# Linear attention into two FFN layers: each head of a pair computes in its own half of the array's columns, the state is kept as diagonal blocks, and the attention's output is cast straight into the FFN's operand

## The chip, the cores and the metric

One core of a Trainium2 chip runs the whole program. The metric is the time on the device in microseconds (us), the median of three runs. The engines are named as the profile names them: PE (TensorE, matmuls; PEld is its loading of weights), DVE (VectorE), ACT (ScalarE), POOL (GpSimd) and SP (SyncE, which here only issues DMAs).

## The reference

Four sequences of 768 steps, 8 heads of 48 features each, pass through an attention with a decaying state; the rows (3072 x 384) then pass through two FFN layers of width 2048.

```python
for t in range(S):
    state = alpha[:, :, t, :, None] * state + np.einsum('bhd,bhe->bhde', k[:, :, t], v[:, :, t])
    y[:, :, t] = np.einsum('bhd,bhde->bhe', q[:, :, t], state)
...
h = x @ w_in;  g = np.maximum(0.01 * h, h);                          x = g @ w_out      # layer 1
h = x @ w_in;  g = np.where(h > 0, h, np.exp(np.minimum(h, 0)) - 1); out = g @ w_out    # layer 2
```

## The kernel before

**Attention.** Time is cut in chunks of 128 steps: 24 units (4 sequences of 6 chunks; `c` is the chunk in its sequence). The 8 heads are 4 pairs (`NP`); the features of a pair's first head lie on partitions 0 to 47, those of the second on 64 to 111 (`PR` = 112). A unit runs through `attn_prep` (products of the decays by two scans on DVE, which scale k and q), `attn_S` (`sc`: scores of each head, on rows 0 to 47 or 64 to 111 of the array; `pk`: k transposed), `attn_S_post` (`A`: masked scores, DVE; `kn`: k copied, ACT; `T`: the old state times the unit's decay), `attn_V` (`po`: output; `pu`: the state's gain) and `attn_V_post`. The state `S` and `T` are [112, 4, 96]: both heads' value columns for every row, of which only the two 48 x 48 blocks on the diagonal are wanted; `mhead`, a column of ones and zeros for each head, clears the others. `vals` holds each pair's values as 48 columns of head 0, 48 zeros and 48 columns of head 1, so that a window of 96 columns that starts at 0 or at 48 places a head's output on rows 0 to 47 or 48 to 95 of `po`.

**Into the FFN.** The FFN wants 384 features as three chunks of 128 partitions (`KD` = 3). Four pairs of 96 features are three chunks of 96 plus a fourth pair, which is cut in three pieces of 32. `attn_V_post` copies `po` into `x32` in that layout with four ACT copies, casts it to `xh` (float32r, ACT), and subtracts to get the rest `xl` (POOL for units 0 to 7, `EARLY_X`, later DVE; `T` likewise with `EARLY_T`).

**FFN.** Every product of layer 1 and 2 is three float32r matmuls (high x high, low x high, high x low). A block is 4 units (512 rows); blocks 0 to 5 of layer 1 run 16 steps each of `ffn1_h` (9 matmuls), `ffn1_g` (ACT, DVE, ACT, DVE) and `ffn1_y` (9 matmuls). While block j runs, the units of block j + 1 run between its steps. `x` tiles have two buffers. The weights come as raw float64 words: `stage1` loads one 128-column step of layer 1 into a slot of `x2t` (four slots), and `convert_p`, `convert_a` and `convert_b` make the high and low parts on ACT and DVE; those of layer 1 run before and during block 0, those of layer 2 during block 5, with rotating pairs of temporaries (`conv_args`: x2t[4] and x2t[5] for layer 1, four pairs of attention tiles for layer 2).

**What sets the order.** Tile's scheduler orders each engine's instructions and places the waits; each engine and each DMA queue then works in its order. PSUM for attention is three banks (`ps_a`), shared by `sc`, `pk`, `po` and `pu`. All loads and stores but one are issued from SP.

## Time and profile before

| | |
|---|---|
| median of 3 runs | 965.43 us (964.12 to 968.95) |
| the profiled execution | 966.94 us, span 965.2 us, granted clock 0.992 |
| PE busy | 931.7 us, 97% of the span |
| DVE, ACT, POOL busy | 57%, 50%, 3% |
| moved by DMA | 54.42 MB, mean 56 GB/s |

The profile is of one execution. PE's busy time counts matmuls in flight, so a busy PE may still run below its best pace; the pace is read from the starts of its rows.

### The profile page before, as it was taken

Reading aid. Unit: us, or ns where it says so; the run is one execution under the profiler, and the core shown is the slowest. Engines: PE = TensorE matmul, PEld = TensorE weight load, DVE = VectorE, ACT = ScalarE, POOL = GpSimd, SP = SyncE. Lnnn points to the kernel's source line nnn. Section 1 sums busy time; section 2 is a strip of 40 time slices with the busy share of each in tenths; the row PEclk is TensorE's granted clock in tenths of the full one; section 3 lists DMA queues with packets and bytes.
Section 4 is the critical chain, followed back from the end, with each engine's and each line's share of the span. In section 5 each row is a group of like instructions: output and inputs, shape, how many; then the busy total and the mean of one; then the engine's idle time right before and its main releaser. Section 6 shows DMA issues by size and latency. Waiting matters only on the chain.

```text
span 965.2 us, 12697 instructions
## 1 busy us (share of the span) xinstructions
PE 931.7 (97%) x4914; PEld 807.6 (84%) x4914; DVE 549.0 (57%) x974; ACT 483.6 (50%) x927; POOL 24.1 (3%) x46
## 2 busy tenths in 40 slices
PE   4889999999999999999999999999999999999997
PEld 3778777888888888888888889989999999999996
DVE  7999999635555557554499973433433433333332
ACT  4566765434334344443488764544544544444442
POOL 0220200000000000000000000000000000000000
PEclk9889999999999999999999999999999999999999
DMA  9445462001112021111144300000000000000001
GB/s 283 124 150 168 130 201 76 1 0 42 42 42 66 18 82 43 42 42 33 55 142 131 115 17 1 6 29 0 33 1 1 34 1 1 33 1 1 34 1 36
DMA packets 17220, 54.42 MB, mean 56 GB/s; under 512 B 1952, under 2 KB 5024, under 8 KB 17152
## 3 DMA queue, kind: packets, MB, share of 16 engines
q1 hardware_dynamic: 17024, 53.31, 17.9%
q8 instruction: 40, 0.66, 0.3%
q14 instruction: 28, 0.23, 0.1%
q10 hardware_dynamic: 128, 0.23, 0.1%
HBM read 48.81 MB, written 4.72 MB: 55 GB/s over the span
## 4 chain that ended last, share of the span: by engine, by line
PE 85%; DVE 10%; DMA 2%; ACT 1%; issue 1%; POOL 0%; SPq 0%; DVEq 0%; ACTq 0%; POOLq 0%
PE hp L312 21%; PE y L283 18%; PE hp L258 18%; PE oa L343 10%; PE o L343 10%; PE po L185 3%; PE sc L155 2%; DMA x2t<-in_w_dram 1%; PE po L188 1%; PE pu L194 1%; DVE x2t L237 1%; DVE E L136 1%; DVE F L140 1%; DVE A L167 1%; DMA pack<-in_seqs_dram 1%
## 5 line engine op out<-in xcount | busy, mean ns | idle before, releaser
L81 DVE TENSOR_TENSOR gl<-t,gh 128x512 fp32r<-128x512 f32 x192 | 132.2, 689 | 109.0 <-ACT gh L78 108.1
L78 ACT CAST gh<-t 128x512 fp32r<-128x512 f32 x192 | 119.1, 621 | 137.6 <-PE oa L343 44.8
L283 PE MATMUL y<-gh,wo 128*128 128x512 f32 x576 | 178.5, 397 | 0.5 <-ACT wo L240 0.5
L321 DVE SCALAR_TENSOR_TENSOR t<-t,hp 128x512 f32<-128x512 f32 x96 | 66.0, 688 | 164.3 <-ACT t L320 164.3
L258 PE MATMUL hp<-xh,wi 128*128 128x512 f32 x576 | 151.2, 395 | 1.2 <-DVE t L267 1.2
L312 PE MATMUL hp<-xh,wi 128*128 128x512 f32 x576 | 149.2, 394 | 0.0
L258 PEld LDWEIGHTS hp<-xh,wi 128*128 128x128 f32 x576 | 107.2, 189 | 24.2 <-ACT wi L240 1.6
L283 PEld LDWEIGHTS y<-gh,wo 128*128 128x128 f32 x576 | 105.7, 188 | 21.9 <-ACT wo L240 1.2
L319 ACT ACTIVATE t<-hp 128x512 f32<-128x512 f32 x96 | 57.3, 597 | 129.1 <-PE hp L312 129.1
L312 PEld LDWEIGHTS hp<-xh,wi 128*128 128x128 f32 x576 | 106.7, 188 | 16.8
L283 PE MATMUL y<-gl,wo 128*128 128x512 f32 x288 | 107.4, 392 | 0.0
L343 PE MATMUL oa<-wo,gh 128*128 128x384 f32 x384 | 98.1, 337 | 0.0
L267 DVE TENSOR_TENSOR t<-t,hp 128x512 f32<-128x512 f32 x96 | 65.3, 680 | 57.3 <-ACT t L266 57.2
L343 PE MATMUL o<-wo,gh 128*128 128x384 f32 x384 | 97.3, 336 | 0.0
L266 ACT ACTIVATE t<-hp 128x512 f32<-128x512 f32 x96 | 57.0, 595 | 78.1 <-PE hp L258 77.6
L312 PE MATMUL hp<-xl,wi 128*128 128x512 f32 x288 | 81.9, 392 | 0.0
L258 PE MATMUL hp<-xl,wi 128*128 128x512 f32 x288 | 81.4, 390 | 0.0
L185 PE MATMUL po<-A,vt 128*96 128x128 f32 x384 | 64.4, 292 | 11.7 <-DVE A L167 11.7
L343 PEld LDWEIGHTS o<-wo,gh 128*128 128x128 f32 x384 | 70.8, 188 | 5.3
L343 PEld LDWEIGHTS oa<-wo,gh 128*128 128x128 f32 x384 | 70.3, 188 | 2.9
L185 PEld LDWEIGHTS po<-A,vt 128*96 128x96 f32 x384 | 52.9, 176 | 16.7 <-DVE A L167 14.0
L312 PEld LDWEIGHTS hp<-xl,wi 128*128 128x128 f32 x288 | 54.1, 188 | 12.5
(106 smaller groups left out, 1124.0 us busy)
## 6 DMA issues: line engine op xcount, KB each, us to landing
pack<-in_seqs_dram SPq DMA_DIRECT2D x23, 674.2 KB, 5.1
x2t<-in_w_dram SPq DMA_DIRECT2D x16, 768.0 KB, 4.9
stg<-in_w_dram SPq DMA_DIRECT2D x28, 384.0 KB, 3.1
vt<-in_vals_dram SPq DMA_DIRECT2D x24, 288.0 KB, 4.5
out_dram<-osb SPq DMA_DIRECT2D x24, 192.0 KB, 1.9
x2t<-in_w_dram SPq DMA_DIRECT2D x4, 384.0 KB, 3.7
pack<-in_seqs_dram SPq DMA_DIRECT2D x1, 226.2 KB, 3.8
pack<-in_seqs_dram ACTq DMA_DIRECT2D x1, 224.0 KB, 4.0
```

Source lines behind the costliest of these rows:

```text
L78: nc.scalar.copy(dst, src)
L81: (lo_engine or nc.vector).tensor_sub(lo, src, dst.bitcast(F32))
L155: nc.tensor.matmul(sc[j][:, p], lhsT=kS[r, p, :], rhs=qh[r, p, :], start=True, stop=True)
L185: nc.tensor.matmul(po[:, p], lhsT=vt[:, p, j * D:j * D + PD], rhs=A[:, j, p], start=(j == 0), stop=(j == 1 and c == 0))
L258: nc.tensor.matmul(hp, lhsT=a[:, kk, :], rhs=x[:, kk, :n], start=(i == 0), stop=(i == 3 * KD - 1))
L266: nc.scalar.activation(t, hp, ACTF.Copy, scale=0.01)
L267: nc.vector.tensor_max(t, t, hp)
L283: nc.tensor.matmul(ytiles[j][c], lhsT=a[:, c * 128:(c + 1) * 128], rhs=x, start=(m == 0 and i == 0), stop=(m == KF - 1 and i == 2),)
L312: nc.tensor.matmul(hp, lhsT=a[:, kk, :], rhs=x[:, kk, :], start=(i == 0), stop=(i == 3 * KD - 1))
L319: nc.scalar.activation(t, hp, ACTF.Relu, scale=-1.0)
L321: nc.vector.scalar_tensor_tensor(out=t, in0=t, scalar=-1.0, in1=hp, op0=ALU.add, op1=ALU.max)
L343: nc.tensor.matmul(otiles[j][i], lhsT=a[:, i * 128:(i + 1) * 128], rhs=x, start=(m == 0 and n == 0), stop=(m == KF - 1 and n == 2),)
```

## The change

Every matmul of `attn_V` is done for each head by itself, with its output on partitions 0 to 47 (or 63) for head 0 and 64 to 111 for head 1, that is in the left or the right 64 columns of the array. `po` is therefore laid out as the heads are, [112, 4, 128]; the matmuls on `T` and for `pu` become 8 for 4. `T` is one constant tile whose blocks off the diagonal are cleared once; only the 48 x 48 blocks are multiplied, and `S` holds those alone ([112, 4, 48]). `mhead` and `x32` are gone. ACT casts `po` into `xh`, DVE subtracts into `xl`; both for every unit, so POOL keeps only a small clearing per unit. The FFN's operand gets a fourth chunk: pairs 0 to 2 lie in chunks 0 to 2 with 16 free partitions behind each head, pair 3 lies in chunk 3, and after the last unit of a block `gather` moves its 96 rows, 16 at a time, into the free partitions: six DMAs for `xh`, six for `xl`. `stage1` brings the rows of w_in into the same order with four DMAs, and w_out with a fifth. Layer 2's conversions have three sets of temporaries for four.

```diff
         if c > 0:
-            T = at_p.tile([PR, NP, PD], F32, tag="T", name="T")
-            (nc.gpsimd if u < EARLY_T else nc.vector).tensor_mul(T, st["S"], d["pe"].to_broadcast([PR, NP, PD]))
-            d["T"] = T
+            for j in range(2):
+                r = slice(64 * j, 64 * j + D)
+                nc.vector.tensor_mul(
+                    T[r, :, j * D:(j + 1) * D], st["S"][r], d["pe"][r].to_broadcast([D, NP, D]))
...
-        po = ps_a.tile([PD, NP, C], F32, tag="at", name="po")
+        po = ps_a.tile([PR, NP, C], F32, tag="at", name="po")
         for p in range(NP):
             for j in range(2):
-                nc.tensor.matmul(po[:, p], lhsT=vt[:, p, j * D:j * D + PD], rhs=A[:, j, p], start=(j == 0),
-                                 stop=(j == 1 and c == 0))
-            if c > 0:
-                nc.tensor.matmul(po[:, p], lhsT=d["T"][:, p, :], rhs=qh[:, p], start=False, stop=True)
+                wide = D if j else 64
+                nc.tensor.matmul(po[64 * j:64 * j + wide, p], lhsT=vt[:, p, 2 * j * D:2 * j * D + wide], rhs=A[:, j, p],
+                                 start=(p == 0), stop=(p == NP - 1 and c == 0), skip_group_check=True)
+        if c > 0:
+            for p in range(NP):
+                for j in range(2):
+                    nc.tensor.matmul(po[64 * j:64 * j + D, p], lhsT=T[:, p, j * D:(j + 1) * D], rhs=qh[:, p],
+                                     start=False, stop=(p == NP - 1), skip_group_check=True)
...
-            pu = ps_a.tile([PR, NP, PD], F32, tag="at", name="pu")
+            pu = ps_a.tile([PR, NP, D], F32, tag="at", name="pu")
             for p in range(NP):
-                vv = vt[:, p].rearrange("s (j e) -> s j e", e=D)[:, 0:3:2, :]
-                nc.tensor.matmul(pu[:, p], lhsT=d["kn"][:, p, :], rhs=vv, start=True, stop=True)
+                for j in range(2):
+                    nc.tensor.matmul(pu[64 * j:64 * j + D, p], lhsT=d["kn"][:, p, 64 * j:64 * j + D],
+                                     rhs=vt[:, p, 2 * j * D:(2 * j + 1) * D], start=(p == 0), stop=(p == NP - 1),
+                                     skip_group_check=True)
...
-        x32 = at_p.tile([128, KD, C], F32, tag="x32", name="x32")
-        nc.scalar.copy(x32[0:PD], po[:, 0:KD])
-        for i in range(KD):
-            nc.scalar.copy(x32[PD:128, i], po[32 * i:32 * i + 32, KD])
+        nc.scalar.copy(xh[0:PR, :, off:off + C], po)
+        nc.vector.tensor_sub(xl[0:PR, :, off:off + C], po, xh[0:PR, :, off:off + C].bitcast(F32))
...
-                    nc.vector.scalar_tensor_tensor(
-                        out=Sn[:, :, cols], in0=pu[:, :, cols], scalar=mhead[:, j:j + 1],
-                        in1=d["T"][:, :, cols], op0=ALU.mult, op1=ALU.add)
+                    nc.vector.tensor_add(Sn[r], pu[r], T[r, :, j * D:(j + 1) * D])
...
-        split(xh[:, :, off:off + C], xl[:, :, off:off + C], x32, nc.scalar, nc.gpsimd if u < EARLY_X else nc.vector)
+
+    def gather(x, n):
+        for b in range(2 * KD):
+            lo, hi = 64 * (b // 3) + 16 * (b % 3), 64 * (b % 2) + D
+            nc.sync.dma_start(x[hi:hi + 16, b // 2, :n].bitcast(F32), x[lo:lo + 16, KD, :n].bitcast(F32))
...
+            if u == blocks[j][0] + blocks[j][1] - 1:
+                for x in (xh, xl):
+                    gather(x, blocks[j][1] * C)
...
-        (eng or nc.sync).dma_start(t, w_words[0][m])
+        w = w_words[0][m]
+        n = 2 * DM
+        for j in range(2):
+            nc.sync.dma_start(t[64 * j:64 * j + D, 0:n], w[D * j:D * j + D, 0:n])
+            nc.sync.dma_start(t[64 * j + D:64 * j + 64, 0:n], w[PD + 16 * j:PD + 16 * j + 16, 0:n])
+        nc.sync.dma_start(t[:, n:], w[:, n:])
...
-            tags = (("T", "S"), ("kn", "x32"), ("E", "F"))[n]
+            tags = (("cT", "S"), ("E", "F"))[n]
```

The scheduler's order moves with it. On PE, early in block 3, unit 16's `po` and `pu` stood between matmuls of `y` in one piece, all in one shape of the array (96 or 112 columns wide, from column 0):

```order
L283 MATMUL y0_2840<-gh_2772,wo1_1_138 128x512
L283 MATMUL y0_2840<-gl_2773,wo0_1_137 128x512
L185 MATMUL po_2869<-A_2805,vt_2380 96x128 x2
L188 MATMUL po_2869<-pack_2378,T_2825 96x128
...
L194 MATMUL pu_2882<-vt_2380,kn_2823 112x96 x4
L283 MATMUL y1_2841<-gh_2772,wo0_1_137 128x512
```

Now the same unit's matmuls alternate between the two halves (64 and 48 columns), and the first stands apart from the others, behind it three matmuls of `y` in the full shape:

```order
L288 MATMUL y2_2979<-gh_2883,wo1_0_136 128x512
L185 MATMUL po_3006<-A_2942,vt_2499 64x128
L288 MATMUL y0_2977<-gl_2884,wo0_0_135 128x512
L288 MATMUL y1_2978<-gl_2884,wo0_0_135 128x512
L288 MATMUL y2_2979<-gl_2884,wo0_0_135 128x512
L185 MATMUL po_3006<-A_2942,vt_2499 48x128
...
L190 MATMUL po_3006<-pack_2497,T_96 48x128 x8
L197 MATMUL pu_3023<-vt_2499,kn_2960 48x48 x8
L288 MATMUL y0_2977<-gh_2909,wo0_1_137 128x512
```

So the array's shape, which changed only around `sc` before, now changes at each piece of `po` and `pu` too. Counted over PE's order from the first `hp` of block 1 to that of block 5, it changes 34 times before and 78 times now; in block 0, 22 and 43 times.

POOL's order around units 2 to 4 was this (`T` for units 3 and 4, `xl` of units 2 and 3, and the clearing of `F`):

```order
L174 TENSOR_TENSOR T_487<-S_422,pe_387 112x384
L81 TENSOR_TENSOR xl_268<-x32_417,xh_267 128x3x128
L131 MEMSET F_639 112x5
L174 TENSOR_TENSOR T_637<-S_512,pe_477 112x384
L81 TENSOR_TENSOR xl_268<-x32_507,xh_267 128x3x128
```

DVE's order at unit 2 now holds both, `xl` between the last step of unit 4's preparation and the state, and `T` behind it:

```order
L141 TENSOR_TENSOR pack_368<-pack_368,F_496 112x512
L207 TENSOR_TENSOR xl_285<-po_414,xh_284 112x4x128
L214 TENSOR_TENSOR S_442<-pu_431,T_96 48x192 x2
L241 TENSOR_SCALAR x2t5_172<-x2t0_167 128x384
L173 TENSOR_TENSOR T_96<-S_442,pe_402 48x4x48 x2
```

On SP, the first block's gathers stand among the pieces of weight loads, each of which waits for its slot of `x2t`:

```order
L422 DMA x2t2_169<-in_w1_dram 48x768
L222 DMA xh_284<-xh_284 16x512 x4
L424 DMA x2t1_168<-in_w1_dram 128x768
L222 DMA xh_284<-xh_284 16x512 x2
L222 DMA xl_285<-xl_285 16x512 x6
L117 DMA vt_560<-in_vals_dram 128x576
```

A weight load there was one DMA before; now a gather may stand behind a piece of one, and the next loads behind the gathers.

## Rows read from the trace of the kernel before

**Rows 1.** The page, part 1 (busy time of each engine, share of the span, instructions) and the chain of work that ended last, by engine.
```profile
PE 931.7 (97%) x4914; PEld 807.6 (84%) x4914; DVE 549.0 (57%) x974; ACT 483.6 (50%) x927; POOL 24.1 (3%) x46
...
PE 85%; DVE 10%; DMA 2%; ACT 1%; issue 1%; POOL 0%; SPq 0%; DVEq 0%; ACTq 0%; POOLq 0%
```

**Rows 2.** Busy time by stretch. The first column is the stretch in us from the span's start, then its length, then busy us (and instructions) of PE, PEld, DVE, ACT and POOL, the granted clock as a share of 2.4 GHz, the DMA share and GB/s. The borders are the first `hp` matmuls of block 0 (57.48), block 1 (158.05), blocks 2 to 5 and of the second layer (551.40).
```profile
0.00:57.48 57.48, 35.49 (x242) 32.12 (x243) 49.23 (x94) 29.95 (x67) 12.00 (x23) 0.89 0.62 189
57.48:158.05 100.57, 96.01 (x562) 78.51 (x562) 95.05 (x197) 67.86 (x150) 10.86 (x11) 0.99 0.46 148
158.05:232.61 74.56, 74.56 (x349) 61.55 (x348) 38.36 (x64) 30.62 (x61) 0.32 (x3) 1.00 0.11 35
...
486.80:551.40 64.60, 64.60 (x287) 53.50 (x285) 62.06 (x132) 51.81 (x107) 0.00 (x0) 1.00 0.43 121
```

**Rows 3.** PE in order of time near the end of block 0: start, length, line, out<-in, records, and in brackets how long PE had idled and for what.
```profile
152.60 0.60 PE L160 MATMUL pk<-ident,pack 112*128 112x112 f32 x4 [2.36 <-DVE A L167]
```

**Rows 4.** PE in order of time around the second half of a unit with a state (unit 13): start, length, line, out<-in, records merged in the row.
```profile
268.42 0.85 PE L258 MATMUL hp<-xl,wi 128*128 128x512 f32 x3
269.11 0.60 PE L185 MATMUL po<-A,vt 128*96 128x128 f32 x4
269.55 0.38 PE L188 MATMUL po<-pack,T 112*96 112x128 f32 x2
...
271.74 0.94 PE L194 MATMUL pu<-vt,kn 128*112 128x96 f32 x8
272.46 0.71 PE L283 MATMUL y<-gh,wo 128*128 128x512 f32 x2
273.01 0.39 PE L283 MATMUL y<-gl,wo 128*128 128x512 f32 x1
```

**Rows 5.** The same view around a run of `sc` matmuls alone, whose two halves use separate rows of the array.
```profile
344.81 0.84 PE L258 MATMUL hp<-xl,wi 128*128 128x512 f32 x3
345.58 1.16 PE L155 MATMUL sc<-pack 48*128 48x128 f32 x16
346.67 0.73 PE L283 MATMUL y<-gh,wo 128*128 128x512 f32 x2
347.24 0.40 PE L283 MATMUL y<-gl,wo 128*128 128x512 f32 x1
```

**Rows 6.** Matmul groups of PE: records in the window 158 to 500 us (first three) and 57.4 to 158 us (last two); busy us and mean ns of one stand behind the bar.
```profile
L185 PE MATMUL po<-A,vt 128*96 128x128 f32 x208 | 30.9, 272 | 0.0
...
L188 PE MATMUL po<-pack,T 112*96 112x128 f32 x88 | 16.9, 272 | 0.0
L194 PE MATMUL pu<-vt,kn 128*112 128x96 f32 x82 | 10.1, 259 | 0.0
...
L185 PE MATMUL po<-A,vt 128*96 128x128 f32 x99 | 16.2, 278 | 0.5 <-DVE A L167 0.5
...
L194 PE MATMUL pu<-vt,kn 128*112 128x96 f32 x47 | 6.2, 260 | 0.0
```

**Rows 7.** Groups of instructions, 0 to 158 us, of POOL and then of ACT: records, busy us, mean ns of one.
```profile
L81 POOL TENSOR_TENSOR xl<-x,xh 128x384 fp32r<-128x384 f32 x8 | 13.3, 1665 | 24.5 <-ACT xh L78 23.9 <-DVE pack L143 0.6
L174 POOL TENSOR_TENSOR T<-S,pe 112x384 f32<-112x384 f32 x6 | 7.4, 1225 | 22.2 <-DVE S L211 16.9 <-DVE S L215 3.5 <-DVE F L132 1.8
...
L204 ACT COPY x<-po 32x128 f32<-32x128 f32 x27 | 6.9, 254 | 0.3
```

**Rows 8.** DVE, then POOL, in order of time: single instructions of 512 and of 384 elements with the one that follows; the first and the last of ten DVE instructions that ran long beside a POOL operation (18.97 and 115.35; an undisturbed one of the first line stands at 37.90); and the POOL operation beside the first.
```profile
12.38 0.69 DVE L142 TENSOR_TENSOR pack<-pack,E 112x512 f32<-112x512 f32 x1
12.98 0.17 DVE L139 RECIPROCAL d<-pe 112x4 f32<-112x4 f32 x1
...
18.05 0.74 DVE L215 TENSOR_SCALAR S<-pu,mhead 112x192 f32<-112x192 f32 x2 [1.70 <-PE pu L194]
...
18.97 1.05 DVE L132 TENSOR_SCALAR F<-pack 112x512 f32<-112x512 f32 x1
...
37.43 0.55 DVE L243 TENSOR_TENSOR wi<-x2t,wi 128x384 fp32r<-128x384 f32 x1
37.90 0.42 DVE L132 TENSOR_SCALAR F<-pack 112x512 f32<-112x512 f32 x1
...
115.35 0.57 DVE L236 TENSOR_SCALAR x2t<-x2t 128x384 int32<-128x384 int32 x1
...
18.88 0.86 POOL L174 TENSOR_TENSOR T<-S,pe 112x384 f32<-112x384 f32 x1 [3.50 <-DVE S L215]
```

**Rows 9.** SP's queue in order of time (one issue), and the DMA issues of the page, part 6 (KB each, median us from issue to landing).
```profile
47.14 0.33 SPq L119 DMA_DIRECT2D vt<-in_vals_dram  x1
...
x2t<-in_w_dram SPq DMA_DIRECT2D x16, 768.0 KB, 4.9
...
out_dram<-osb SPq DMA_DIRECT2D x24, 192.0 KB, 1.9
```

**Rows 10.** PE around two block borders: the last `po` of unit 3 and the first `hp` of block 0; the last `po` of unit 15 and the first `hp` of block 3.
```profile
46.95 0.38 PE L188 MATMUL po<-pack,T 112*96 112x128 f32 x2
...
57.48 3.27 PE L258 MATMUL hp<-xh,wi 128*128 128x512 f32 x10
...
310.35 0.38 PE L188 MATMUL po<-pack,T 112*96 112x128 f32 x2
...
317.50 1.52 PE L258 MATMUL hp<-xh,wi 128*128 128x512 f32 x6
```

More of the change, by code (lines that the diff above doesn't have):

```diff
@@ L63, in attention_two_layers_kernel @@
     causal = const.tile([128, C], F32, name="causal")
-    mhead = const.tile([PR, 2], F32, name="mhead")
+    T = const.tile([PR, NP, PD], F32, name="T")
     d0 = const.tile([PR, EXT], F32, name="d0")
@@ L90, in constants @@
         )
-        for j in range(2):
-            nc.vector.memset(mhead[:, j:j + 1], 0.0)
-            nc.vector.memset(mhead[64 * j:64 * j + D, j:j + 1], 1.0)
+        nc.gpsimd.memset(T, 0.0)
         nc.vector.memset(d0, 0.0)
@@ L200, in attn_V_post @@
         po = d["po"]
[L201 to L204 removed]
+        nc.scalar.copy(xh[0:PR, :, off:off + C], po)
+        nc.vector.tensor_sub(xl[0:PR, :, off:off + C], po, xh[0:PR, :, off:off + C].bitcast(F32))
         if c < NC - 1:
             pu = d["pu"]
[L207 removed]
+            Sn = at_p.tile([PR, NP, D], F32, tag="S", name="S")
             for j in range(2):
[L209 removed]
+                r = slice(64 * j, 64 * j + D)
                 if c > 0:
[L211 to L213 removed]
+                    nc.vector.tensor_add(Sn[r], pu[r], T[r, :, j * D:(j + 1) * D])
                 else:
[L215 removed]
+                    nc.vector.tensor_copy(Sn[r], pu[r])
             st["S"] = Sn
[L217 removed]
+    def gather(x, n):
+        for b in range(2 * KD):
+            lo, hi = 64 * (b // 3) + 16 * (b % 3), 64 * (b % 2) + D
+            nc.sync.dma_start(x[hi:hi + 16, b // 2, :n].bitcast(F32), x[lo:lo + 16, KD, :n].bitcast(F32))
     w_words = [w1.bitcast(I32), w2.bitcast(I32)]
@@ L373, in xtile @@
             xt[j] = (
-                xs_p.tile([128, KD, 512], F32R, tag="xh", name="xh"),
-                xs_p.tile([128, KD, 512], F32R, tag="xl", name="xl"),
+                xs_p.tile([128, KD + 1, 512], F32R, tag="xh", name="xh"),
+                xs_p.tile([128, KD + 1, 512], F32R, tag="xl", name="xl"),
                 n,
@@ L433, in conv_args @@
         w = (wout if i else win)[m]
-        n = nconv[0] % 4
+        n = nconv[0] % (4 if layer == 1 else 3)
         nconv[0] += 1
@@ L438, in conv_args @@
             tp, ts = tt[:, 0:384], tt[:, 384:768]
-        elif n == 3:
+        elif n == 2:
             tt = at_p.tile([128, 768], I32, tag="A", name="cA")
@@ L529, in weights @@
                 for i, w in enumerate((win[m], wout[m])):
-                    tp, ts = [at_p.tile([128, 384], I32, tag=n, name=f"c{n}") for n in ("kn", "x32")]
+                    tp, ts = [at_p.tile([128, 384], I32, tag=n, name=f"c{n}") for n in ("kn", "cT")]
                     args = t[:, i * 768:i * 768 + 768], tp, ts, flat(w[0]), flat(w[1])
```

5 lines of the change are left out of this document (1 added, 4 removed).

## The prediction

> **What bounds the kernel now.** I read the page first: PE is busy for 97% of the span and holds 85% of the chain that ended last [rows 1]. A busy PE need not be a full one, so the stretches come next [rows 2]. From 158.05 us on PE never idles, at full clock, and DVE is busy for about half of the time (38 of 75 us in block 1); only in block 5, where layer 2's weights are converted, does DVE come near (62.06 of 64.60), and PE still does not wait. What PE gets rid of there comes off the time one for one. Block 0 is another stage: in 100.57 us DVE is busy 95.05, PE 96.01, and near its end PE idles 2.36 us for the masked scores `A` from DVE [rows 3]. Two engines share that bound, so work taken from one of them may give nothing. Before 57.48 us DVE (49.23 of 57.48) works through the units' preparation, PE is mostly waiting, its clock at 0.89 of full speed in the mean. So the change is priced in three stages against the profiled 966.94 us, which is 1.5 us over the median of 965.43. A difference below 0.5% (4.8 us) I take as no change.
>
> **PE, blocks 1 to 4.** A float32 matmul leaves two records. In a unit with a state, 24 records of `po` stand between 269.11 and 271.74: 0.11 us each [rows 4]. Before them three `hp` take 0.23 each (268.42 to 269.11); the run ends two `y` ahead of 273.01, at 272.56. So `pu` takes 0.82 for 8 records, and the borders of the run cost almost nothing.
>
> What two matmuls side by side cost is seen at `sc`, whose two heads use separate rows of the array [rows 5]. Its slot runs from 345.49 (three `hp` after 344.81) to 346.79 (two `y` ahead of 347.24): 1.30 us for 16 records, where one after the other at 0.11 would take 1.75. Abreast they are 8 steps of 0.11, 0.88; the other 0.42 are the two changes of the array's shape, 0.21 each.
>
> The new `po` and `pu` are pairs in separate columns. No row shows such a pair; the nearest is the pair in separate rows, and I take its step.
> - Scores part of `po`: 16 records become 8 steps, 0.88 saved. The window from 158 us on has 208 such records [rows 6], 13 units: -11.4 us.
> - State part: 8 records before, 16 now in 8 steps: nothing. It is worth 0.88 more for each of 88/8 = 11 units if the pairs do not run abreast.
> - `pu`: 8 records of 0.10, now 16 of half the columns in 8 steps. A step costs between 0.05 (half of one) and 0.11 (the pair's step above); 0.07 is a middle value, since half the columns halve the streaming but not the issuing. 82 records are 10 units: -2.6 us, ends -4.2 and +0.6.
> - Changes of shape: 44 more in these blocks (78 for 34, from the order). At 0.21 that is +9.2 us. The lower end is the border of [rows 4], nearly nothing; I take the row with a real change of shape.
>
> Sum -4.8 us; ends -15.6 (no price for the shape, the cheap `pu`) and -1.6.
>
> **Block 0.** PE: 99 records are 6.2 units, -5.4; `pu` 47/8 x 0.26 = -1.5; 21 more changes of shape +4.4: -2.5 in all. DVE: POOL's `xl` and `T` move to it. Of POOL's 8 and 6 [rows 7], four and two are among its 11 instructions after 57.48 [rows 2]; the other five clear `F`. A DVE instruction of 512 elements takes 0.60 to the next one (12.38 to 12.98), one of 384 takes 0.47 (37.43 to 37.90) [rows 8]; by that line one of 192 takes 0.27. `xl` is now 512 wide: 4 x 0.60 = 2.4. `T` is twice 192: 2 x 0.54 = 1.1. Against it stand DVE instructions that POOL stretched: at 18.97 one of line 132 took 1.05 beside POOL's `T`, an undisturbed one 0.42 [rows 8]. Ten such ran 4.4 us over the usual length of their lines, two of them, 0.6 us together, in block 0. So DVE gains 2.9 us of work where it is 95% busy, and PE loses 2.5. I take 0, ends -2.5 and +2.9.
>
> **Before block 0.** DVE gets four `xl` (2.4) and four `T` (2.2) and loses 3.8 of stretching: +0.8. On the way of the state DVE waits for PE, 1.70 us before unit 0's `S` [rows 8]; the shorter `po` and `pu` run shortens this for each of the first units. ACT loses the copies into `x32`, three of them 0.25 each [rows 7], which stood ahead of `xh`. I take -1, ends -2 and +0.8.
>
> **The gathers.** Each of the 12 DMAs holds SP for 0.33 us, and a small store lands 1.9 us after issue [rows 9]: `xh` is whole some 0.6 (cast) + 6 x 0.33 + 1.9 = 4.5 us after the block's last `po`, `xl` 2 us later. Cover: the scheduler puts two groups of `y` and one of `hp` between, 7.1 us from 310.35 to 317.50 [rows 10], and the new order some matmuls of `y` more; `xl` is used 1.4 us later still. At block 0 the last `po` at 46.95 and the first `hp` at 57.48 leave 10.5. So 0. If the cover were gone, it would be the 2 us of a landing at each of five borders, +10.
>
> **SP.** A weight tile takes five issues for one: 64 more, 21 us of SP, and 24 for all gathers, on a queue that mostly waits for free slots. What stands behind a piece that waits comes late: a load lands 4.9 us after its issue [rows 9]. I take 0, the upper end one such landing on DVE's or PE's way, +5. It can gain too: the piece for w_in no longer waits for the slot of w_out.
>
> **Hidden.** ACT's lighter load is off the way from 158 us on (PE never waits there). Three sets of temporaries for layer 2's conversions are covered by block 5's PE work [rows 2] and by the first block of layer 2, which uses the last weights at its end; without that cover, a set held for one more DVE round, under 2 us. 0.
>
> **Sum.** -4.8 + 0 - 1 = -5.8, so 961.1 us on the profiled execution's scale and 959.6 on the median's; the round 960 is my forecast, at the edge of what can be told from no change.
>
> **Rivals.**
> 1. *The shape of the array changes at little cost for columns.* Then the 9.2 us stay in the pocket: -15 us, 950. For it: the two shapes differ only in columns, and widths 96, 112 and 128 already follow one another free [rows 4]. Against: `sc` pays 0.21 each way [rows 5]. Chance 0.16.
> 2. *The halves do not run abreast* (the other side). Place: the `po` and `pu` runs. Per pair of records before, 24 x 0.11 in a unit with a state; after, 16 steps. The break-even is a step of 0.135 us: from there on the changes of shape eat everything. If the records simply follow one another, the scores part gains nothing, the state part costs 0.88 x 11 = 9.7, the changes 9.2: +19, or 984. For it: these pairs read the same rows, `sc`'s pairs do not, and nothing in the trace runs abreast on one set of rows. Against: weights are loaded behind running matmuls everywhere here. The Trainium skill (TensorE: Matmul & The Clock Gate, Part 3: Packing small matmuls) says that a load of weights overlaps running matmuls only when the row group differs, and on its figures three column tiles of another kernel still ran 2.38 times as fast as one after the other; by the first alone the result would lie towards 984, by the second near the forecast, and no run here has shown column tiles yet. Chance 0.12.
> 3. *DVE keeps block 0, and the finer weight loads come late behind gathers* on SP: +2.9 and one landing of 4.9 in front of a conversion, with the -4.8 elsewhere and no gain before block 0: +3, 968. For it: DVE's 95.05 of 100.57. Chance 0.14, half of it in the no-change band, half above.
> 4. *A border waits for its gather*, at several borders: +10 - 5.8, so 970. Chance 0.06, a third of it no change.
>
> The forecast itself (pairs abreast, shapes dear) has 0.52, own range 955 to 966.
>
> **How the numbers follow.** Faster is below 960.6: 0.29 of the forecast's 0.52 and rival 1, 0.45. Same: the forecast's other 0.23, 0.07 and 0.02, 0.32. Slower: 0.12 + 0.07 + 0.04 = 0.23. The range takes in rival 1 and 3 and leaves most of 2 out: 949 to 973.
>
> **What would show it.** In a unit with a state, `po` should take 16 starts in pairs some ns apart, 0.11 per pair, the whole run about 2.7 us for 3.45; `pu` 8 pairs of 0.05 to 0.11. Starts 0.11 apart one by one mean rival 2. The first `y` behind such a run tells the price of the shape. Block 0 should last 98 to 104 us, with POOL empty and no DVE instruction stretched. PE should not idle at the first `hp` of blocks 1 to 5; an idle there ended by a DMA on `xh` or `xl` is rival 4. Wrong I would be above all by the step of a pair and by the price of a change of shape, the two that no row shows for columns.

## The result, and the profile after

The changed kernel takes 977.71 us, the median of four runs (973.16 to 980.14), against 966.31 for the kernel before beside it: 1.0104 times as long, 95% interval 1.0080 to 1.0129. It is slower; the forecast was 960.0, with a range of 949 to 973. Its profiled execution is the quickest of the four, 973.16 us with a span of 971.1 and a granted clock of 0.983 (966.94, 965.2 and 0.992 before), so what is read from it below shows 6.2 us of the 11.4 between the two medians.

First the page, part 1 and the chain by engine [answers rows 1].

```profile
PE 926.9 (95%) x5234; PEld 787.3 (81%) x5234; DVE 558.2 (57%) x1004; ACT 455.0 (47%) x831; POOL 4.4 (0%) x33
...
PE 87%; DMA 6%; DVE 4%; SPq 1%; ACT 1%; issue 1%; DVEq 0%; ACTq 0%
```

PE is busy 4.8 us less in a span that is 5.9 us longer. In the chain DVE fell from 10% to 4% and DMA rose from 2% to 6%. Next the stretches, cut at the same places, the first `hp` of blocks 0, 1, 2 and 5 and of layer 2 [answers rows 2].

```profile
0.00:60.58 60.58, 33.33 (x276) 28.60 (x277) 50.11 (x101) 25.48 (x51) 2.13 (x16) 0.86 0.74 196
60.58:164.69 104.11, 95.50 (x617) 73.45 (x618) 97.88 (x203) 62.04 (x129) 0.98 (x5) 0.94 0.51 139
164.69:244.52 79.83, 79.83 (x418) 64.45 (x417) 42.36 (x71) 28.29 (x51) 0.32 (x3) 0.99 0.13 38
...
492.69:557.93 65.24, 63.76 (x281) 52.49 (x280) 56.93 (x120) 46.67 (x96) 0.00 (x0) 1.00 0.40 117
```

Block 2 starts at 244.52 for 232.61: the first three stretches lose 11.9 us. Length less PE's busy time is PE's idle time: 27.25 and 8.61 in the first two, 35.9 in all, against 21.99 and 4.56, 26.6, before. So 9.3 of the 11.9 are idle PE; the other 2.6 are a PE that was busy longer although its attention runs are shorter. In block 0 its granted clock is 0.94 for 0.99. From 159.50 to 166.30 us, across the border of block 1 and after waits of 2.05 and 0.90 us, it stands at 0.50, the lower of its two levels (1.2 GHz):

```profile
159.50:166.30 6.80, 5.90 (x18) 4.37 (x17) 6.80 (x16) 1.95 (x4) 0.00 (x0) 0.50 0.00 0
```

PE is busy for 5.90 us there; at the full clock that would be half, some 3 us less (an estimate), a good part of what is missing. Blocks 2 to 4 give some of it back. Their sums, three blocks together, before and then after (length, then busy time of each engine):

```profile
sum 254.19, PE 254.19 PEld 213.94 DVE 145.96 ACT 107.87 POOL 0.97; mean PE 84.73 PEld 71.31 DVE 48.65 ACT 35.96 POOL 0.32
```

```profile
sum 248.17, PE 248.17 PEld 200.95 DVE 148.41 ACT 92.64 POOL 0.97; mean PE 82.72 PEld 66.98 DVE 49.47 ACT 30.88 POOL 0.33
```

That is 6.0 us less, and PE never waits there. The changed order also puts five more FFN matmuls inside these borders (870 records for 865, 1.1 us). Where it comes from is seen in a unit with a state (PE in order of time) [answers rows 4].

```profile
279.70 0.84 PE L263 MATMUL hp<-xl,wi 128*128 128x512 f32 x3
280.47 1.09 PE L185 MATMUL po<-A,vt 128*64 128x128 f32 x16
281.39 1.05 PE L190 MATMUL po<-pack,T 112*48 112x128 f32 x16
282.27 0.53 PE L197 MATMUL pu<-vt,kn 128*48 128x48 f32 x16
282.73 0.73 PE L288 MATMUL y<-gh,wo 128*128 128x512 f32 x2
```

Three `hp` at 0.23 us end at 280.39; the first `y` starts at 282.73, so the run takes 2.34 us. Before, by the same two starts, it is 3.35 (269.11 to 272.46 [rows 4]); the forecast's 3.45 put the end two `y` ahead of a later start, and by that measure the run is now 2.45. Either way it is 1.0 us shorter. Sixteen records of `po` take 0.92 (280.47 to 281.39): 8 pairs of 0.11. `pu` takes 0.46 (282.27 to 282.73), 8 pairs of 0.06, for 0.72 before (271.74 to 272.46).

Now the loss at the start. SP's queue, the packs of units 2 and 3, before and then after:

```profile
4.79 0.33 SPq L114 DMA_DIRECT2D pack<-in_seqs_dram  x1
...
12.41 0.33 SPq L114 DMA_DIRECT2D pack<-in_seqs_dram  x1
```

```profile
11.06 0.43 SPq L112 DMA_DIRECT2D pack<-in_seqs_dram  x1
...
20.73 0.42 SPq L424 DMA_DIRECT2D x2t<-in_w_dram  x1
21.33 0.31 SPq L112 DMA_DIRECT2D pack<-in_seqs_dram  x1
```

They leave 6.3 and 8.9 us later, behind the pieces of the weight tiles. Each DMA waits for the semaphore of the one eight issues ahead of it, so a tile in five pieces fills most of what may be under way. What DVE waited for up to 165 us (total us, times, longest), before and after:

```profile
DVE F L132 <- DMA pack<-in_seqs_dram: 3.6, 2, 2.3
```

```profile
DVE F L130 <- DMA pack<-in_seqs_dram: 11.7, 5, 4.0
```

And the border of block 0 in the changed kernel: ACT's cast of the last unit's `xh`; SP's queue behind it; the first `hp` on PE; the DMAs issued from 50 to 66 us, with KB and median us to landing.

```profile
53.28 0.57 ACT L206 CAST xh<-po 112x512 fp32r<-112x512 f32 x1
```

```profile
54.26 2.50 SPq L222 DMA_DIRECT2D xh<-xh  x4
56.86 0.53 SPq L424 DMA_DIRECT2D x2t<-in_w_dram  x1
57.44 2.40 SPq L222 DMA_DIRECT2D xh<-xh  x2
59.93 4.02 SPq L222 DMA_DIRECT2D xl<-xl  x6
```

```profile
60.58 2.04 PE L263 MATMUL hp<-xh,wi 128*128 128x512 f32 x4 [3.79 <-ACT pack L131]
```

```profile
pack<-in_seqs_dram SPq DMA_DIRECT2D x1, 674.2 KB, 6.0
...
xh<-xh SPq DMA_DIRECT2D x6, 32.0 KB, 4.7
xl<-xl SPq DMA_DIRECT2D x6, 32.0 KB, 1.9
```

A gather holds SP for some 0.6 us. By itself it lands 1.9 to 2.0 us after its issue, as the six of `xl` do here; those of `xh` take 4.5 us in the median of all blocks (36 transfers) because they stand behind loads that were issued just ahead of them. In the trace's landings the pack issued at 53.33 lands at 59.31, the piece of a weight tile issued at 53.75 at 59.91, and the four gathers issued from 54.26 on at 60.12, 60.30, 60.49 and 60.68. At the border of block 5, where the loads ahead had landed by 488.92, the last two of `xh` took 1.96. Here the last of `xh` lands at 61.61 and the last of `xl` at 65.30: 8.3 and 12.0 us after the cast began, where the forecast had 4.5 us for `xh` and 2 more for `xl`. The 3.79 us before `hp` stand against an ACT instruction that `hp` does not read; its end happens to lie there (59.87 and 0.72), and the landing of the first gathers does too.

### The profile page after: what moved, and what is told of

Same layout as the page of the kernel before. It is cut to its first block, busy times and chain, and to the rows that moved or that the text cites. A ratio compares the mean times of both kernels' runs of the same rounds, so it can differ in the third digit from the quotient of the medians.

```text
span 971.1 us, 13446 instructions
## 1 busy us (share of the span) xinstructions
PE 926.9 (95%) x5234; PEld 787.3 (81%) x5234; DVE 558.2 (57%) x1004; ACT 455.0 (47%) x831; POOL 4.4 (0%) x33
## 4 chain that ended last, share of the span: by engine, by line
PE 87%; DMA 6%; DVE 4%; SPq 1%; ACT 1%; issue 1%; DVEq 0%; ACTq 0%
PE hp L317 21%; PE y L288 19%; PE hp L263 19%; PE oa L348 10%; PE o L348 10%; DMA x2t<-in_w_dram 3%; PE sc L153 2%; PE po L185 2%; DMA pack<-in_seqs_dram 2%; PE po L190 1%; DMA vt<-in_vals_dram 1%; PE pk L158 1%; DVE x2t L242 1%; DVE x2t L244 1%; PE pu L197 1%
## 5 line engine op out<-in xcount | busy, mean ns | idle before, releaser
L326 DVE SCALAR_TENSOR_TENSOR t<-t,hp 128x512 f32<-128x512 f32 x96 | 66.0, 687 | 164.7 <-ACT t L325 164.7
L288 PEld LDWEIGHTS y<-gh,wo 128*128 128x128 f32 x576 | 106.2, 189 | 26.6 <-ACT wo L245 3.0
L324 ACT ACTIVATE t<-hp 128x512 f32<-128x512 f32 x96 | 57.4, 598 | 125.9 <-PE hp L317 125.9
L271 ACT ACTIVATE t<-hp 128x512 f32<-128x512 f32 x96 | 56.1, 593 | 57.6 <-PE hp L263 57.5
L348 PE MATMUL oa<-wo,gl 128*128 128x384 f32 x192 | 64.3, 338 | 0.0
L317 PEld LDWEIGHTS hp<-xl,wi 128*128 128x128 f32 x288 | 54.1, 188 | 12.5
L348 PE MATMUL o<-wo,gl 128*128 128x384 f32 x192 | 63.4, 337 | 0.0
```

Of the source, the lines that this page charges most:

```text
L271: nc.scalar.activation(t, hp, ACTF.Copy, scale=0.01)
L288: nc.tensor.matmul(ytiles[j][c], lhsT=a[:, c * 128:(c + 1) * 128], rhs=x, start=(m == 0 and i == 0), stop=(m == KF - 1 and i == 2),)
L317: nc.tensor.matmul(hp, lhsT=a[:, kk, :], rhs=x[:, kk, :], start=(i == 0), stop=(i == 3 * KD - 1))
L324: nc.scalar.activation(t, hp, ACTF.Relu, scale=-1.0)
L326: nc.vector.scalar_tensor_tensor(out=t, in0=t, scalar=-1.0, in1=hp, op0=ALU.add, op1=ALU.max)
L348: nc.tensor.matmul(otiles[j][i], lhsT=a[:, i * 128:(i + 1) * 128], rhs=x, start=(m == 0 and n == 0), stop=(m == KF - 1 and n == 2),)
```

## The experiments

All of them are timed against the kernel before on the same chip. "One-piece" is the changed kernel with a weight tile in one DMA. The starts are the first `hp` of blocks 0, 1 and 2 in the profiled execution.

| kernel | median us | ratio to before, 95% interval | starts of blocks 0, 1, 2 |
|---|---|---|---|
| before | | | 57.5, 158.1, 232.6 |
| changed | 977.7 | 1.0104 (1.0080 to 1.0129) | 60.6, 164.7, 244.5 |
| one-piece (e_onew) | 969.5 | 1.0024 (1.0012 to 1.0037) | 62.8, 162.4, 240.4 |
| one-piece, no gathers (e_onew_nogather) | 959.3 | 0.9910 (0.9890 to 0.9930) | 55.5, 155.9, 234.0 |
| changed, no gathers (e_after_nogather) | 964.0 | 0.9970 (0.9948 to 0.9992) | 55.3, 160.1, 239.2 |
| one-piece, gathers to DRAM (e_onew_dram) | 960.9 | 0.9928 (0.9910 to 0.9947) | 54.3, 159.1, 237.1 |
| before, five pieces (e_before_split) | 965.5 | 0.9981 (0.9966 to 0.9997) | 54.1, 156.6, 228.6 |
| before, T and xl on DVE (e_before_dve) | 963.2 | 0.9965 (0.9947 to 0.9984) | 46.6, 152.7, 226.6 |
| the same, five pieces (e_dve_split) | 964.1 | 0.9968 (0.9949 to 0.9987) | 51.1, 152.6, 230.7 |

**The weight tiles in one piece.** The host orders the rows of w_in as the partitions are.

```diff
-        for j in range(2):
-            nc.sync.dma_start(t[64 * j:64 * j + D, 0:n], w[D * j:D * j + D, 0:n])
-            nc.sync.dma_start(t[64 * j + D:64 * j + 64, 0:n], w[PD + 16 * j:PD + 16 * j + 16, 0:n])
-        nc.sync.dma_start(t[:, n:], w[:, n:])
+        (eng or nc.sync).dma_start(t, w_words[0][m])
```

> The changed kernel, with the rows of the first layer's input weights laid out on the host in the order of the new partitions, so that each weight tile comes in one DMA again and not in five. The gathers stay. Theory A (SP's queue: five pieces per weight tile, with eight DMAs in flight, hold back the packs and weights of the first 165 us): 77 fewer issues before block 1, pack of unit 2 issued by about 5 us again (after: 11.06) and that of unit 3 by about 13 us (after: 21.33); first hp of block 0 back to 57 to 58 us, that of block 1 to 156 to 160 us, and the time 6 to 13 us under the changed kernel's 977.7, so 965 to 972, at or below the kernel before. Theory B (VectorE's added xl and T set block 0): first hp of block 1 stays near 165 us and the time within 2 us of the changed kernel's. Theory C (the short attention matmuls or a lower granted clock cost it, wherever the loads are): the same as B.

Measured: 0.8% less than the changed kernel (1.0104 to 1.0024), 7.7 us. The time and the packs of units 2 and 3 (4.94 and 12.53 us) are where theory A has them, but the first `hp` of block 0 is no earlier (62.8), which A did not expect, and that of block 1 (162.4) is late for its 156 to 160.

**The five pieces alone, in the kernel before** (the same rows in pieces of 48, 16, 48 and 16 partitions, then the other half).

> The kernel before, with nothing changed but that each first-layer weight tile comes in the five pieces of the changed kernel (48, 16, 48 and 16 partitions of the input half, then the output half); what lands is the same. Theory A: slower than the kernel before by 5 to 9 us (971 to 975), with the packs of units 2 and 3 issued 6 to 9 us later and the first hp of block 1 at 163 to 167 us. Theory B or C: within 1.5 us of the kernel before, first hp of block 1 at 157 to 160 us.

Measured: 0.9981, if anything quicker. Yet the packs are as late as in the changed kernel (11.71 and 22.60 us); DVE's waits up to 165 us:

```profile
DVE F L132 <- DMA pack<-in_seqs_dram: 9.4, 4, 4.2
```

Theory A falls in its simple form: 5.8 us more of waiting for packs cost this kernel nothing.

**T and xl on DVE, in the kernel before** (`EARLY_T, EARLY_X = 0, 0`).

> The kernel before, with T and xl of the first eight units on VectorE instead of GpSimd, and nothing else. Theory A: within 2 us of the kernel before, since the stretched VectorE instructions go with GpSimd's work. Theory B: slower by 4 to 8 us, block 0 105 us or longer (100.6 before).

Measured: 0.9965, so 3.4 us quicker. Block 0 grows to 106.0 us, as theory B has it, but it starts 10.8 us earlier, and the time goes the other way: in the kernel before, what the change put on DVE is by itself a gain. The windows, to be laid beside [rows 2]:

```profile
0.00:46.65 46.65, 29.80 (x221) 26.89 (x221) 39.84 (x83) 25.39 (x57) 1.67 (x14) 0.96 0.70 216
46.65:152.67 106.02, 97.98 (x588) 79.53 (x587) 106.02 (x222) 72.70 (x160) 0.73 (x6) 0.98 0.47 152
```

DVE does 145.9 us of work up to block 1 for 144.3 before, but the stretch is 5.4 us shorter: that the waits behind POOL's long instructions were dearer than the work is the likely reason. This kernel beats both.

**Gathers from ScalarE's queue**, one-piece (`nc.scalar.dma_start` in `gather`).

> As the changed kernel with one-piece weight tiles, and the gathers issued from ScalarE's queue instead of SP's. Theory A with the gathers as the second part of it (12 gathers at a border, each waiting for a landing eight issues before, ahead of the packs): 1 to 3 us under the one-piece kernel, no pack late at the borders. If the gathers cost SP nothing: within 1.5 us of it, or 1 to 2 us above for 12 issues of some 0.3 us on ScalarE at each border.

Measured: 1.0093, 6.7 us above the one-piece kernel, far over both expectations. The gathers land no earlier: their median for `xh` is 4.7 us, and the first two, issued at 53.16 and 53.80, land at 57.89 and 58.07, right behind the pack that SP issued at 52.54 (57.69). What ACT's conversions lost behind the gathers was not separated.

**TensorE kept at work before block 0**, one-piece.

```diff
+        def warm(rhs):
+            w = ps_y.tile([128, C], F32, tag="y2", name="warm")
+            for g in range(2):
+                for p in range(NP):
+                    nc.tensor.matmul(w, lhsT=ident[:rhs.shape[0], :], rhs=rhs[:, p, :], start=True, stop=True)
```

> The one-piece version of the changed kernel, with 8 further matmuls of 128x128 after each of the two TensorE halves of units 0 to 3 (64 in all, into an accumulator bank that nothing reads before the first y), so that TensorE has work where it waited for VectorE; the outputs are the same. In the one-piece kernel the granted clock is 0.50 to 0.77 from 30 to 66 us, where TensorE is busy 1.2 to 5.8 of each 6 us; in the kernel before it is 0.58 to 1.00 there. Theory D (the shorter attention runs leave TensorE idle at the start, its clock falls to the lower level, and attention and the first FFN matmuls run at half speed): clock above 0.9 from 30 to 66 us, first hp of block 2 4 us or more earlier (one-piece: 240.4), time 963 to 966. Theory B (VectorE's own work sets block 0, the clock costs nothing there): the clock rises and the first hp of block 2 stays within 2 us, time 967 to 972.

Measured: 1.0018, no change. From 30 to 66 us, one-piece and then this kernel (the clock is the third figure from the end):

```profile
30.00:66.00 36.00, 23.31 (x188) 19.05 (x187) 33.18 (x67) 14.48 (x30) 0.43 (x4) 0.62 0.45 141
```

```profile
30.00:66.00 36.00, 30.67 (x301) 25.83 (x301) 32.63 (x69) 12.90 (x27) 0.32 (x3) 0.95 0.50 145
```

The clock rose from 0.62 to 0.95, block 0 starts at 56.6 for 62.8, and block 2 starts at 240.2 for 240.4. The lower clock before block 0 follows from PE's waiting; it is not what costs there. Theory D falls.

**No gathers**, one-piece: the transfers are taken out, and rows 96 to 127 are cleared first.

> The one-piece version without the gathers: the 16 rows of each half of the FFN's operand that they would fill hold zeros, or whatever the attention wrote there, so two heads are left out of the first layer. If the gathers cost only at block 0's first border, as a late start (4.5 us landing): first hp of block 0 3 to 6 us earlier than 62.8 and the time 1 to 4 us under the one-piece kernel's 969.5. If they hold SP's queue and with it packs and weights all the way: 4 to 8 us under it. If they are hidden, as forecast: within 1 us.

Measured: 0.9910, that is 1.14% or 11 us under the one-piece kernel, more than any expectation. The last cast of `xh` begins at the same place (53.06 us, one-piece with gathers 52.77), but the first `hp` follows 2.5 us later and not 10.1. Block 0 starts 7.3 us earlier, block 2 6.4 us earlier, and blocks 2 to 4 are quicker as well:

```profile
sum 244.83, PE 244.83 PEld 200.22 DVE 150.29 ACT 92.97 POOL 6.68; mean PE 81.61 PEld 66.74 DVE 50.10 ACT 30.99 POOL 2.23
```

```profile
sum 248.43, PE 248.43 PEld 200.89 DVE 148.10 ACT 92.70 POOL 0.97; mean PE 82.81 PEld 66.96 DVE 49.37 ACT 30.90 POOL 0.32
```

The second row is the one-piece kernel: 3.6 us more, with PE never idle in either. Of these, 1.1 us are five FFN matmuls that its order puts inside the three blocks (869 records for 864). The rest goes with the attention, which the scheduler cuts into 11, 11 and 10 runs between FFN matmuls, where it has 9, 9 and 9 without gathers: 10 more changes of the array's shape, some 0.25 us each with the pairs that a cut takes apart. That the scheduler does so to have a block's last unit done a landing earlier is a reading of the order. In block 5 the one-piece and the changed kernel also have a wait that the kernel without gathers does not have; in the changed kernel:

```profile
500.68 1.66 PE L263 MATMUL hp<-xh,wi 128*128 128x512 f32 x6 [1.48 <-DVE t L272]
```

**Attention's output copied out of PSUM first**, one-piece (ACT copies `po` to an SBUF tile; `xh` and `xl` are made from it).

> The one-piece version with po copied by ScalarE to an SBUF tile first, and xh and xl made from the copy, so that po's PSUM bank is free after the copy and not only after VectorE's xl (in the one-piece kernel TensorE's pk waits 4.8 us for xl in block 0, longest 2.7 us). Theory E (banks held by xl slow the early units): 2 to 5 us under the one-piece kernel, the waits of pk for xl gone. Otherwise within 1.5 us of it; ScalarE has 13 more instructions of 0.6 us in block 0, at 60% busy.

Measured: 1.0088, 6 us worse, though the wait of `pk` for `xl` is gone. Theory E falls, and the other expectation (within 1.5 us) as well; PE waited 17.1 us for `A` instead of 11.6.

**One head after the other**, one-piece (the loops over `p` and `j` in `attn_V` exchanged).

> The one-piece version with the matmuls of po and pu in another order: all of the first head's, then all of the second's, so that no two with different columns stand side by side. If the pairs run abreast as read from the trace of the changed kernel: the wall of po and pu goes from 2.46 us to 4.1 us or more, blocks 2 to 4 each grow from about 82.8 to 89 us, and the time rises by 20 us or more, less what the cover in blocks 0 and 1 takes. If the shorter runs come from the narrower matmuls alone: within 3 us of the one-piece kernel.

Measured: 1.0156, 13 us worse. But blocks 2 to 4 take 254.13 us for 248.43, 5.7 more or 0.5 a unit, where one matmul of 0.11 after another would add 0.88 for each half of `po`. The rows of a unit say why (line 185 is the scores part, 190 the state part; the first row holds 8 records of the left half and 5 of the right):

```profile
285.07 1.24 PE L185 MATMUL po<-A,vt 128*64 128x128 f32 x13
286.04 0.31 PE L190 MATMUL po<-pack,T 112*48 112x128 f32 x1
286.15 0.27 PE L185 MATMUL po<-A,vt 128*48 128x128 f32 x1
286.19 0.27 PE L190 MATMUL po<-pack,T 112*48 112x128 f32 x1
```

The scores of the second head still run while the state part of the first has begun. In the single starts the first head's matmuls stand alone from 285.07 to 285.56, some 0.11 apart, that is as dear as full ones; from 285.56 on one of the second head starts beside each of the rest. So the exchange took only a part of the pairs asunder, and it does not show that narrower matmuls are cheaper by themselves: what ran alone was not. The rest of the 13 us lies before block 2, which starts at 248.8. Neither expectation holds whole.

**The changed kernel without gathers; gathers that nobody waits for; gathers from GpSimd; gathers in two parts.**

> The changed kernel with its five-piece weight tiles, and without the gathers (the 16 rows of each half of the FFN's operand hold zeros or what the attention wrote there, so two heads are left out of the first layer). With one-piece tiles the gathers cost 10.2 us (969.5 against 959.3). Theory F (the two add up, each holding SP by itself): 977.7 less 10, so 966 to 969. Theory G (five pieces cost only behind gathers, since in the kernel before they cost nothing): 958 to 962, the same as without gathers and with one-piece tiles.

> The one-piece version in which the 12 transfers of each border are issued at the same place on SP, from the same rows, but go to a DRAM scratch tensor, so that no matmul waits for them (rows as in the run without gathers; two heads left out). If the price of 10.2 us is SP's queue (12 issues in order, ahead of packs and weights): 966 to 970, as with the gathers. If it is the wait of the block's first hp for the last landing, and the order that follows from it: 958 to 962, as without them.

> The one-piece version with the gathers issued by GpSimd, which has no other work there, instead of SP. If SP's queue is the price: 959 to 964. If the wait for the landing is: 966 to 971, or more if GpSimd needs longer for an issue than SP's 0.6 us; on ScalarE's queue, which has work of its own, it was 976.3.

> The one-piece version with two gathers per block: the columns of its first three units after the third unit, those of the last after the fourth (24 transfers per block instead of 12, the last 12 of a third of the size). If the price is the wait for the landing of large transfers: 2 to 4 us under the one-piece kernel's 969.5. If it is the number of issues on SP: 2 to 6 us above it. If it is a fixed latency of the last 12 issues and a landing: within 1.5 us.

Measured, in that order: 0.9970, 0.9928, 1.0152 and 1.0031. Without gathers the five pieces still cost 0.6%, 5.8 us (0.9970 to 0.9910): theory G falls, and F holds roughly, as the gathers cost 13 us beside five pieces and 11 beside one. The same twelve issues at each border, to DRAM, cost 1.7 us (0.9928 to 0.9910, with intervals that overlap, so it may be nothing): SP's queue is at most a small part of the gathers' price, and blocks 2 to 4 are as long as without gathers (244.82 us). The rest, some 9 us, comes with an operand that waits for them. From GpSimd they are dearer by 12 us. Smaller last gathers gain nothing. Neither the issuing engine nor the size makes the landing shorter: from GpSimd

```profile
xh<-xh POOLq DMA_DIRECT2D x36, 32.0 KB, 5.4
```

and the last ones of a third of the size

```profile
xh<-xh SPq DMA_DIRECT2D x36, 8.0 KB, 3.8
```

stand behind the same loads: GpSimd's first gather, issued at 55.31, lands at 58.52, the pack that SP issued at 53.25 at 58.30. No run has the gathers ahead of the pack.

**Does POOL's slack hide the five pieces in the kernel before? And the paired matmuls with the right output and no gathers.** In e_padded the fourth pair's heads are written by matmuls with padded operands:

```diff
+            for j in range(2):
+                b = 2 * p + j
+                nc.tensor.matmul(po[64 * j:64 * j + 64, p], lhsT=v6[:, b], rhs=A[:, b // KD, KD],
+                                 start=(p == 0), stop=False, skip_group_check=True)
```

> The kernel before with T and xl of the first eight units on VectorE (963.2 with one-piece weight tiles) and its weight tiles in the five pieces of the changed kernel. The five pieces cost the kernel before nothing (965.5 against 966.6), and the changed kernel 4.8 us without gathers (964.0 against 959.3). Theory H (they make the packs late in every kernel, VectorE's wait for packs going from 3.6 to 9.4 us; in the kernel before this lies in time in which VectorE waits for GpSimd's chain anyway, and is bare where VectorE has taken that chain over): 4 to 6 us over the one-piece time, so 967 to 970. If the pieces cost only beside the paired matmuls or the order that comes with them: within 1.5 us of 963.2.

> The paired matmuls without gathers and with the right output: the heads of the fourth pair are written by matmuls, not by transfers, into the 16 rows of each half (their v and their state stand in 64-column operands whose first 48 columns are zero), one-piece weight tiles. It has 4 more pairs of matmuls in po (2 for the scores, 2 for the state), xh and xl of 384 columns instead of 512, two small ScalarE copies for the state's operand, no transfer before an FFN matmul, and v tiles of 816 columns instead of 576. If the wait for the gathers is the price: 959.3 plus some 0.4 us in each of 12 units that lie where TensorE is the limit, so 961 to 966, under the kernel before. If the paired matmuls themselves hold the first block back: 968 or more.

Measured: 0.9968, so no cost there either, and theory H falls. The padded kernel: 1.0002. It starts block 0 at 47.8 and block 2 at 233.3, 7.1 us earlier than the one-piece kernel, but its longer runs take blocks 2 to 4 to 254.18 us, as before the change: 0.78 us a unit for four more pairs (254.18 to 244.83 over 12 units), where 0.4 had been expected. The time lies between the two expectations.

**Padded operands in block 0, gathers later; the five pieces from GpSimd.**

> The paired matmuls, one-piece weight tiles, and the two ways of filling the 16 rows in one kernel: block 0's four units by matmuls with padded operands (no transfer before the first FFN matmul), all later units by the gathers; three conversion temporaries instead of four make room for the padded state. By the blocks measured: block 2 starts at 233.3 with padded operands throughout, of which four units of block 1's time cost some 3 us that fall away, so about 230 to 231; then 248.4 to block 5 and 478.4 to the end as in the one-piece version with gathers: a span of 957 to 959 and a time of 958 to 962, under the kernel before and at or under 963.2, the kernel before with T and xl on VectorE. If the gather's wait at the first border is not what costs: 966 to 970.

> The changed kernel with its five-piece weight tiles issued by GpSimd instead of SP; gathers and packs stay on SP. If the five pieces cost 8.2 us because packs and gathers queue behind them on SP: 968 to 972, VectorE's waits for packs back from 11.7 to about 6 us. If they cost it by landing late themselves, or by GpSimd's slower issue: 976 or more.

Measured: 1.0038 and 1.0232. The mixed kernel has its first `hp` at 48.5, 14 us earlier than the one-piece kernel, and loses all of it in block 0:

```profile
48.47:168.43 119.96, 104.25 (x674) 76.45 (x673) 117.36 (x241) 70.56 (x146) 0.95 (x8) 0.94 0.47 142
```

It also has one conversion temporary less, so it does not show cleanly that the first border is free; it does show that an early first `hp` alone is no gain. The second run settles nothing: GpSimd's own queue held the first unit up.

```profile
DVE F L130 <- POOL F L129: 20.7, 2, 20.5
```

**Work taken from DVE** (the last subtraction of each layer-1 conversion goes to GpSimd).

```diff
-        nc.vector.tensor_sub(lo, ts.bitcast(F32), hi.bitcast(F32))
+        (nc.gpsimd if nconv[0] <= 2 * KF else nc.vector).tensor_sub(lo, ts.bitcast(F32), hi.bitcast(F32))
```

> The one-piece version of the changed kernel, gathers and all, with the last subtraction of each of the 32 first-layer weight conversions (the low part, 128x384, 0.55 us on VectorE, 17.5 us in all) on GpSimd, which is idle there and took 1.0 us for a subtraction of this form in the kernel before. In fourteen of the seventeen profiles so far block 2 starts 66 to 70 us after the end of the last conversion on VectorE, however early the first hp is, and VectorE is 90% busy until then. Theory B (VectorE's sum of work and waits up to the last conversion sets the time): the last conversion ends 8 to 14 us earlier than 173.2, less what GpSimd stretches, and the time is 957 to 963. Theories A and F (the late first hp, packs and gathers set it): within 3 us of 969.5.

> The kernel before with T and xl of the first eight units on VectorE (963.2) and the last subtraction of each first-layer conversion on GpSimd, as above. Theory B: 951 to 958. If VectorE isn't the limit there: within 3 us of 963.2. Without VectorE as the limit the shorter paired matmuls should show: the paired version of this call then lies at or under this one.

Measured: 0.9990, 3.3 us under the one-piece kernel, and 0.9959, the same as without it; the paired kernel does not come under the unpaired one. The last step of a conversion that both have on DVE (L244) ends 16 us earlier (154.0 for 169.9), and block 2 starts only 3.5 us earlier (236.9): DVE's sum of work is a small part of it, and theory B falls for good. With DVE freed, the first `hp` now shows what it waits for:

```profile
PE hp L263 <- DMA xh<-xh: 2.5, 1, 2.5
```

## Why the prediction was wrong

**What held.** Two matmuls in separate columns do start side by side: a pair of `po` takes the 0.11 us taken from `sc`, so rival 2 (984) is out. The Trainium skill (TensorE: Matmul & The Clock Gate, Part 3: Packing small matmuls) lets a load of weights overlap running matmuls only where the row group differs; here pairs that read the same rows run at 0.11 a pair, so the measurement decides for its other statement, the measured gain of column tiles. `pu` pairs take 0.06, the cheap end, and 0.26 less a unit, as forecast. A change of shape is not free for columns, and somewhat cheaper than forecast: without gathers blocks 2 to 4 gain 9.4 us (254.19 to 244.83); 12 units at 0.88 and 10 at 0.26 for `pu` would be 13.2, and the missing 3.8 over the 26 further changes there (54 for 28 in the order) are 0.15 each, for 0.21 forecast. This is a price by difference, and `pu`'s 0.46 already holds a part of the change behind it. Rival 1 (950) is out as it stands. With gathers and pieces both taken away the kernel is 0.9% quicker than before, 8.7 us for the 5.8 of the sum, but not where the sum has it: blocks 2 to 4 gain 9.4, and block 2 starts 1.4 us later (234.0 for 232.6) and not earlier.

**The step that failed first: "So 0" for the gathers.** They cost 11 us (13 beside five pieces). It failed in three places. An issue took 0.6 us where the row of a load had 0.33 [rows 9]. A landing alone takes the 1.9 us taken from the store, but the gathers of `xh` stood behind a pack that takes 5 to 6 us, and took 4.5 in the median: a load ahead of them was not in the term at all. The cover of 10.5 us at block 0 [rows 10] was no idle time to hide in: between the two rows PE works on the next unit and waits for `A`, as these rows of the kernel before show,

```profile
51.53 0.46 PE L185 MATMUL po<-A,vt 128*96 128x128 f32 x2 [1.54 <-DVE A L167]
53.25 0.74 PE L185 MATMUL po<-A,vt 128*96 128x128 f32 x2 [1.26 <-DVE A L167]
```

and without gathers the first `hp` came 2.5 us after the last cast of `xh` began. And a border with cover still pays: PE does not idle at the first `hp` of blocks 1 to 5, as forecast, but the order that goes with it has more, shorter runs, some 2.5 us in three blocks, and a wait of 1.48 us inside block 5. Rival 4 named the mechanism; its size (+10) was luck, since it was added up from an idle PE at five borders, and PE idles for a landing at block 0 only. It had 0.06 because I looked for it there.

**The step that failed second: "I take 0" for SP.** The five pieces cost 5.8 us, 7.7 beside gathers; the upper end was 5. That packs and not only weights stand behind a piece was not thought of: they leave SP 6 to 9 us later. The sum of the two steps, 18.7 us by the ratios, is what lies between -8.7 and the +10 measured.

**Block 0 and before.** DVE's added work was taken as 0 and -1, and no run shows that it did the harm: moving T and xl to DVE in the kernel before gained 3.4 us, and taking 32 subtractions off DVE in the one-piece kernel gained 3.3. Rival 3 (968) had the late pieces right and DVE wrong. Block 0 took 104.1 us, just outside the 98 to 104 named.

**What stays open.** The five pieces make DVE wait 5 to 6 us longer for packs in every kernel, but only the paired kernels become slower (5.8 and 7.7 us, against -1.8 and +0.3 in the unpaired ones). POOL's work does not explain it, and the run that took the pieces off SP was held up at its own start. The scheduler gives each kernel another order, and the paired kernels tend to a lower clock in block 0 (0.93 to 0.99, unpaired 0.97 to 1.00), so order and clock may both be in it; neither was separated. For the same reason, how the gathers' first border turns into 6 us at block 2 is not settled: the operand that depends on the gathers is shown to be the cause, by the gathers to DRAM; an early first `hp` alone is not the cure, since block 2 starts no earlier for it with the further matmuls (56.6 for 62.8, block 2 at 240.2).

## What to carry to other kernels

A short transfer between two steps of the pipeline is priced by its issues one behind the other, by its own landing (here 1.9 us) and by what is under way ahead of it (here a pack of 674 KB, 5 to 6 us), whichever engine issues it. "Cover" counts only if the engine would otherwise idle in it: work that fills the gap has to be done anyway. Where a scheduler sets the order, a hidden latency can still show as more and shorter runs. A layout that saves matmul time should be charged for every DMA that it adds to a queue that other loads share, and for what those loads feed.

## What was not expected of the hardware

Two heads in separate columns run side by side even where the kernel's loops name all of the first head's matmuls ahead of the second's: a unit lost 0.5 us by that order, where one after the other would have cost 0.88 for each half of `po`. The records of 64-column matmuls without a partner stood 0.11 apart, as those of 96 columns do. A transfer of 32 KB from GpSimd's or ScalarE's queue landed behind a load that SP had issued, as it did from SP's own. GpSimd's subtraction of 128x384 took 1.3 to 1.7 us in long series beside a busy DVE (mean ns behind the bar, one-piece kernel with that work on GpSimd):

```profile
L248 POOL TENSOR_TENSOR wo<-x2t,wo 128x384 fp32r<-128x384 f32 x16 | 22.5, 1408 | 38.9 <-ACT wo L245 38.9
```

and in the kernel before it took 1.67 in the mean [rows 7]. Taking it off GpSimd there, with `T`, was worth more than it cost DVE (0.55 us for one of 384 elements).
